# Who makes the high halves: w2's chunks from ScalarE to VectorE, probabilities from tile 16 on from GpSimd to VectorE

## The chip, the cores and the metric

One core of one Trainium2 chip. The metric is the device time of one execution in microseconds (us); for the kernel before it is the median of three runs. The engines are named as the profile names them: PE (TensorE matmul), PEld (its weight load), DVE (VectorE), ACT (ScalarE), POOL (GpSimd) and SP (SyncE, which issues most of the DMAs).

## The reference, cut to what matters

Three stages run one after the other, on a batch of two, with sequence 768 and model width 512. The first is an attention over 8 heads of 64, masked by the equality of hash buckets:

```python
q_bits = (np.einsum('bhsd,dk->bhsk', q, proj) > 0)      # 6 bits, so a bucket number
mask = q_bucket[:, :, :, None] == k_bucket[:, :, None, :]
scores = np.where(mask, scale * q @ k.T, -1e9)
attn = softmax(scores); x = attn @ v
```

The second adds a two-dimensional Fourier transform, normalises and applies a two-layer perceptron: `u = x + real(fft2(x))`, `un = layernorm(u)`, `x = u + relu(un @ w_ch1) @ w_ch2`, where w_ch1 is 512 x 2048 and w_ch2 2048 x 512. The third mixes tokens: `theta = x @ w_theta`, then the sequence sums of `x cos(theta)` and `x sin(theta)` with two 768 x 768 weights, and `u + relu(u @ w_ch)`.

The weights arrive as 64-bit floats, so each weight is first rebuilt as a 32-bit float in the kernel. To keep the accuracy of 32 bits, most operands of a matmul are split into a high half (the value rounded to 16 bits, or to the PE's reduced 32-bit form) and a low half (the value less the high half), and three products are summed. The change concerns who makes high halves.

## The kernel before, in words

**Weights.** `conv16` (line 183) turns a weight into two 16-bit halves, 512 columns at a time. For each chunk `from_f64` (line 169) loads 512 KB of 64-bit words into a buffer `r` (three of them, `NCV`, line 167) by a DMA on SP's queue; ACT runs two operations on it (lines 177 and 179), DVE joins the parts with one scalar_tensor_tensor (line 180, the tile `r` again). Then ACT copies the result into the high half (line 187, `w2h<-r` for w2) and POOL subtracts to get the low half (line 188, `w2l<-r,w2h`). The buffer is free for the next load when POOL is done. w2 has 16 such chunks, each used by the matmuls of one value of `fi` in `mlp2` (line 799).

**Attention of batch 1.** `attention` (line 416) goes over 4 pairs of heads, 2 heads in each, and 6 tiles of 128 query rows in each: 48 tiles, counted by `n`. For a tile, PE makes the scores (`pss`), DVE takes the row maximum (`attn_max`, line 349, a TENSOR_REDUCE into `nm`), ACT takes the exponential (`attn_exp`, line 353) into a 128 x 768 tile of 32-bit floats `p`. `attn_split` (line 361) makes the high half in the tile `p2` on ACT or POOL, by the pattern `h1`, and the low half on POOL (`l1`). A DMA transpose on SP's queue turns both halves (`transposed`, line 379), and PE multiplies them with the values into `pso` (`attn_AV`). Since the buffers of these tiles are shared, the profile names them `p`, `pt` or `x`. The pattern is "aapap", so of each five tiles ACT makes three high halves and POOL two, those with `n % 5` equal to 2 or 4: 19 of the 48.

**Order.** The engines run their instructions strictly in the order in which they were issued. That order comes from the scheduler of the tile framework (line 1178), which plans with modelled durations, the due times set by `at` and `timed` (for w2's chunks 100 us and one more for each, line 968; for the tiles of batch 1 115 us and 2.6 more for each, line 969), and the gates set by `after_gate`. So the two conversions, the tiles of batch 1 and the perceptron of batch 0 (`mlp`, lines 971 and 976) are interleaved: while attention of batch 1 runs, PE also runs `mlp1` and `mlp2` of batch 0, whose evacuations need ACT (`hh<-psm`) and DVE (`hl<-psm,hh`). All instructions that the scheduler places late carry the line of a helper, L62 or L64, so the profile is read by tiles. After the last tile of batch 1 come its Fourier transform, its perceptron and the third stage.

Of the kernel before, what the change touches and what calls it, by code (L numbers as in the profile page):

```python
# [15 lines left out]
AF = mybir.ActivationFunctionType  # L16
# [5 lines left out]
DM, DFF = 512, 2048  # L22
# [15 lines left out]
def run(g):  # L38
    for _ in g:
        pass  # L40
# [30 lines left out]
def fused_kernel(ctx, tc, A, out):  # L71
    nc = tc.nc
    V, AC, PE, PL, SY = (Ordered(tc, e) for e in (nc.vector, nc.scalar, nc.tensor, nc.gpsimd, nc.sync))
# [4 lines left out]
    def mk(p, shape, dt, tag, **kw):  # L78
        return p.tile(shape, dt, tag=tag, name=tag, **kw)
# [4 lines left out]
    def pl_copy(out, in_, scale=1.0):  # L84
        PL.tensor_scalar(out=out, in0=in_, scalar1=scale, scalar2=0.0, op0=ALU.mult, op1=ALU.add)

    def stt(eng, out, in0, in1, op, scale=1.0):
        if eng is V:
            return V.scalar_tensor_tensor(out=out, in0=in0, scalar=scale, in1=in1, op0=ALU.mult, op1=op)
        assert scale == 1.0  # L90
        return eng.tensor_tensor(out=out, in0=in0, in1=in1, op=op)

    T = dict(
        pet='dpd', dup=1, c2=0, c0=46, cx=0, wm=6, gf=1, o2=0, xs=1, sb=2, al=[['p', 2], ['p2', 3], ['pt', 3]], cs='v', g0=1,
        lg=[[0, 2], [2, 4], [4, 6]], ub=2, pace0=1.6, lead=60, f0=50.0, w1=60.0, w1s=1.0, b1=115, pace1=2.6,
        w2=100.0, w2s=1.0, m0=170.0, f1=190.0, th=240.0, m1=290.0, z0=330.0, wt=300.0, n0=8, n1=16, k0=12, k1=16, c1=46, tp=16, i0=40, i1=[20, 10],
        ne=42, es=150, ld='ss', lc='s', ps=[[0, 3], [0, 5], [1, 0], [1, 5]])
# [17 lines left out]
    def PS(k):  # L115
        n = turn[k] % sum(c for _, c in ring[k])
        turn[k] += 1
        for p, c in ring[k]:
            if n < c:
                w = [128, 2, 512] if k == "s" else [128, 512]  # L120
                tag = "psm" if p in [x[0] for x in ring["m"]] else "ps" + k
                live[k] = p.tile(w, F32, tag=tag, name=tag)
                return live[k]
            n -= c
# [4 lines left out]
    def at(us):  # L129

        tc.cur_priority = int(1000 * us)
# [20 lines left out]
    def fill(n, k="o"):  # L152

        for _ in range(n):
            PE.matmul(live[k][:, 392:512], pat[:, 0], pat[:, 1, 0:120], start=True, stop=True)
# [13 lines left out]
    def from_f64(src, scale=1.0, n=CN):  # L169
        p = cvs[turn["cv"] % len(cvs)]  # L170
        turn["cv"] += 1
        r = mk(p, [128, 2 * CN], U32, "r64", bufs=NCV if p is cv_p else None)
        r = r[:, 0:2 * n]
        {"s": SY, "a": AC, "p": PL}[T["lc"]].dma_start(out=r, in_=src.bitcast(U32))
        lo, hi = r[:, 0:2 * n:2], r[:, 1:2 * n:2]

        AC.activation(out=lo, in_=lo, func=AF.Relu, scale=2.0 ** -29 * (1 - 2.0 ** -20), bias=c_half)

        AC.activation(out=f(hi), in_=f(hi), func=AF.Prelu, scale=scale * 2.0 ** -112, alpha=2.0 ** 32)
        V.scalar_tensor_tensor(out=lo, in0=hi, scalar=3, in1=lo, op0=ALU.logical_shift_left, op1=ALU.bitwise_or)  # L180
        return f(lo)

    def conv16(src, n, hi, lo, lo_eng):
        for i in range(n // CN):
            c = slice(CN * i, CN * i + CN)
            w = from_f64(src[:, c], 2.0)
            AC.activation(out=hi[:, c], in_=w, func=AF.Copy)
            stt(lo_eng(i), lo[:, c], w, hi[:, c], ALU.subtract)
            yield

# [28 lines left out]
    def soft_tile(k):  # L219
        n = turn[k] % len(soft[k])  # L220
        turn[k] += 1
        return soft[k][n]
# [116 lines left out]
    def attn_S(st, t):  # L339
        ps = PS("s")  # L340
        c = slice(128 * t, 128 * t + 128)
        for k in range(2):
            for g in range(2):
                mm(ps[:, g, 0:384], st[:, k, c], st[:, 2 + k, 384 * g:384 * g + 384], k == 0, k == 1)
        return ps
# [7 lines left out]
    def attn_exp(ps, nm=None):  # L353
        m = None
        if nm is None:
            nm, m = attn_max(ps)
        p = soft_tile("p")[:, 0]
        e = AC.activation(out=two3(p), in_=ps[:, :, 0:384], func=AF.Exp, bias=nm)
        return p, [m, e]

    def attn_split(p, p2, hi_eng, lo_eng):
        if hi_eng is AC:
            AC.activation(out=p2[:, 0], in_=p, func=AF.Copy)
        else:
            pl_copy(p2[:, 0], p)
        return stt(lo_eng, p2[:, 1], p, p2[:, 0], ALU.subtract)
# [12 lines left out]
    def transposed(p2):  # L379
        pt = soft_tile("pt").bitcast(F16).rearrange("p a n -> p (a n)").rearrange("p (k n) -> p k n", n=128)  # L380
        m = SY.dma_start_transpose(out=pt, in_=p2.bitcast(F16).rearrange("p a n -> p (a n)"))
        return pt, m

    def attn_AV(o, pt, vv, hh, t):
        for k in range(6):
            mm(o[:, t], pt[:, k], vv[:, 0, hh, k], k == 0, False)
            mm(o[:, t], pt[:, k], vv[:, 1, hh, k], False, False)
            mm(o[:, t], pt[:, 6 + k], vv[:, 0, hh, k], False, k == 5)
# [20 lines left out]
    def after_gate(b):  # L409

        es = ExitStack()
        for m in [] if b is None else [b] if hasattr(b, "ins") else gate[b] if isinstance(gate[b], list) else [gate[b]]:
            es.enter_context(tc.issue_after(m.ins))
        return es

    def attention(b, t0, pace, lead, hi_eng, lo_eng, after=lambda b, j: None):
        x_t[b] = mk(x_p, [128, NT, DM], F32, "x")
        n, w = 0, soft["p2"][0].shape[1]
        for j in range(4):
            i = 4 * b + j  # L420
            if i not in made:
                at(t0 + pace * n - lead)
                with after_gate("p1" if b else None):
                    run(prep(b, j))
            st, vv = made[i]
            for hh in range(2):
                h = PO[j] + 4 * hh
                at(t0 + pace * n)
                o = PS("o")[:, 0:NT * (D + 1)].rearrange("p (t d) -> p t d", t=NT)
                for t in range(NT):  # L430
                    at(t0 + pace * n)
                    ps = attn_S(st[hh], t)
                    fill(T["i1"][n] if n < len(T["i1"]) else 0)
                    with after_gate(0 if b and n >= T["n1"] else "ln0" if b and n >= T["n0"] else None):
                        p, m = attn_exp(ps)
                    if not t % w:
                        p2 = soft_tile("p2")
                    with after_gate(0 if b and n >= T["n1"] else None):
                        attn_split(p, p2[:, t % w].bitcast(F16).rearrange("p (a n) -> p a n", a=2), hi_eng(n), lo_eng(n))
                    if t % w == w - 1:  # L440
                        pt, trans = transposed(p2)
                        for i in range(w):
                            attn_AV(o, pt[:, 12 * i:12 * i + 12], vv, hh, t - w + 1 + i)
                    n += 1
                    if j < 3 and [hh, t] in T["ps"]:
                        at(t0 + pace * n - lead)
                        if [hh, t] == T["ps"][0]:
                            new = prep(b, j + 1)
                        next(new)
                at(t0 + pace * n - 30)  # L450
                attn_norm(b, h, o)
            after(b, j)
# [320 lines left out]
    w1, w2 = {}, {}  # L773
# [145 lines left out]
    def timed(gen, t0, dt):  # L919
        n = 0  # L920
        while True:
            at(t0 + dt * n)
            if next(gen, gen) is gen:
                return
            n += 1

    ev = lambda s: [AC if c == "a" else PL if c == "p" else V for c in s]
    h1, l1, c1, c2 = (ev(k) for k in ("aapap", "p", "p", "p"))
    pick = lambda e, last=None: lambda n: last if last and n >= T["ne"] else e[n % len(e)]
    at(0.2)  # L930
    run(prep_pair(0, True))
    at(T["f0"] - 40)
# [32 lines left out]
        timed(take(cw1, T["k1"] - T["k0"]), T["f0"] + 1, T["w1s"])  # L965
    with after_gate(0):
        timed(cw1, T["f0"] + 1, T["w1s"])
        timed(conv16(A["w2"], 16 * DM, w2[0], w2[1], pick(c2)), T["w2"], T["w2s"])
    attention(1, T["b1"], T["pace1"], T["lead"], pick(h1), pick(l1))

    def mlp(b, t0, gs):
        for g in gs:
# [212 lines left out]
```

## Time and profile before

| | us |
|---|---|
| median of 3 runs (729.09 to 731.25) | 729.41 |
| the profiled execution | 728.28 |
| its span, first to last instruction | 726.5 |
| PE busy (matmuls) | 664.8, 92% of the span |
| DVE busy | 402.6, 55% |
| ACT busy | 372.7, 51% |
| POOL busy | 370.1, 51% |

The profiled execution took 1.8 us more than its span, and 1.1 us less than the median. A busy PE is the union of its matmuls, whose ends are modelled, so 92% is an upper bound of its real use. The shares of the other engines are averages over stages: attention and weight conversion fill the first half of the span, the perceptron of batch 1 and the token mixing the second, where PE works almost without a gap and the others idle.

### The profile page before, as it was taken

To read this page: it belongs to the slowest core of one execution; us is meant where nothing else is said; L and a number is where in the kernel's file an instruction comes from. 1 tells how busy PE (TensorE), PEld (TensorE's weight loads), DVE (VectorE), ACT (ScalarE), POOL (GpSimd) and SP (SyncE) were. 2 spreads that over 40 slices of the span, in tenths; PEclk is the share of its full clock that TensorE was granted. 3 is DMA by queue.
4 is the path that set the end of the run, shared out by engine and by line. 5 is a ranking of instruction groups with operands and counts; after the bars stand their busy time and mean duration, and the time that the engine had idled before them with its cause. 6 is when DMAs were issued, how large, how long until landed. Compare 5 with 4: busy or idle time off the path is not lost.

```text
span 726.5 us, 13450 instructions
## 1 busy us (share of the span) xinstructions
PE 664.8 (92%) x5424; PEld 510.9 (70%) x5424; DVE 402.6 (55%) x655; ACT 372.7 (51%) x597; POOL 370.1 (51%) x312
## 2 busy tenths in 40 slices
PE   5798988669668898999999999999999899999998
PEld 2365556557557655786686786687485599999997
DVE  1566787865999665543377583255422476751222
ACT  2565565766988898773423152065325676730010
POOL 3787789586878888776660020033403446930000
PEclk9999999978699999999999999999999999999999
DMA  9896967459889999776560043011004631720202
GB/s 327 186 187 141 157 121 142 93 164 213 197 206 240 269 231 253 151 145 124 102 195 27 13 120 65 1 45 30 1 1 145 223 89 39 234 81 25 88 1 87
DMA packets 161469, 93.68 MB, mean 129 GB/s; under 512 B 137088, under 2 KB 147584, under 8 KB 161408
## 3 DMA queue, kind: packets, MB, share of 16 engines
q1 hardware_dynamic: 159472, 86.27, 51.3%
q0 software_dynamic: 1936, 6.57, 2.6%
q8 instruction: 42, 0.69, 0.4%
q14 instruction: 19, 0.16, 0.1%
HBM read 49.82 MB, written 6.29 MB: 77 GB/s over the span
## 4 chain that ended last, share of the span: by engine, by line
PE 48%; POOL 10%; issue 9%; DMA 6%; ACT 5%; DVE 4%; POOLq 0%; SPq 0%; DVEq 0%; ACTq 0%
PE psm L62 31%; PE psf L62 14%; POOL p L62 3%; ACT r L62 2%; PE pso L62 2%; POOL w1l L62 2%; DMA x<-p 2%; POOL stk L62 2%; PE pss L62 1%; DMA r<-in_wtok 1%; DMA r<-in_w 1%; POOL pt L62 1%; DVE r L62 1%; ACT stk L62 1%; POOL w2l L62 1%
## 5 line engine op out<-in xcount | busy, mean ns | idle before, releaser
L62 PE MATMUL psm<-unT,w1h 128*128 128x256 f16 x768 | 130.4, 274 | 0.1
L62 PE MATMUL psm<-unT,w1l 128*128 128x256 f16 x384 | 105.2, 274 | 0.0
L62 DVE SCALAR_TENSOR_TENSOR r<-r 128x512 uint32<-128x512 uint32 (+1 forms) x64 | 64.6, 1016 | 51.9 <-ACT r L62 49.2
L62 PEld LDWEIGHTS <-w1h 128*128 128x128 f16 (+1 forms) x774 | 75.1, 99 | 15.5 <-issue 4.5
L62 PEld LDWEIGHTS <-hh 128*128 128x128 f16 x384 | 37.1, 98 | 42.8 <-issue 2.2
L62 POOL TENSOR_TENSOR w1l<-r,w1h 128x384 fp32r<-128x384 f32 (+1 forms) x36 | 41.9, 1178 | 43.5 <-ACT w1h L62 43.5
L62 PE MATMUL pss<-stk 128*128 128x384 f32 x192 | 48.8, 384 | 15.2 <-ACT p L62 9.4
L64 PE MATMUL pss<-stk 64*128 64x384 f32 (+1 forms) x288 | 55.4, 470 | 6.4 <-ACT p L64 3.2
L62 DVE TENSOR_REDUCE nm<-pss 128x1 f32<-128x768 f32 x48 | 44.9, 949 | 29.0 <-PE pss L62 28.8
L62 PE MATMUL psm<-w2h,hl 128*128 128x512 f16 x192 | 60.3, 379 | 0.0
L62 PE MATMUL psm<-w2l,hh 128*128 128x512 f16 x192 | 59.8, 379 | 0.2 <-POOL w2l L62 0.2
L62 ACT ACTIVATE r<-r,chalf 128x512 uint32<-128x512 uint32 (+1 forms) x64 | 46.1, 720 | 26.2 <-DMA r<-in_wtok 10.2
L62 PE MATMUL psm<-w2h,hh 128*128 128x512 f16 x192 | 59.3, 379 | 0.0
L62 POOL TENSOR_TENSOR p<-p,p 128x768 f16<-128x768 f32 x32 | 54.7, 1715 | 6.6 <-ACT p L62 5.5
L62 ACT ACTIVATE p<-pss,nm 128x768 f32<-128x768 f32 x48 | 42.5, 892 | 28.1 <-DVE nm L62 23.3
L62 DVE SCALAR_TENSOR_TENSOR hl<-psm,hh 128x512 f16<-128x512 f32 x48 | 32.8, 687 | 41.9 <-ACT hh L62 41.8
L64 DVE TENSOR_REDUCE nm<-pss 128x1 f32<-128x768 f32 x48 | 43.6, 950 | 19.9 <-PE pss L64 19.8
L62 ACT ACTIVATE hh<-psm 128x512 f16<-128x512 f32 x48 | 28.2, 590 | 40.4 <-PE psm L62 40.4
L62 PEld LDWEIGHTS pss<-stk 128*128 128x128 f32 x192 | 34.6, 204 | 20.2 <-ACT p L62 11.9
L62 PEld LDWEIGHTS <-w1l 128*128 128x128 f16 x384 | 37.7, 98 | 5.7 <-issue 1.2
L62 ACT ACTIVATE r<-r 128x512 f32<-128x512 f32 (+1 forms) x64 | 39.5, 618 | 0.0
L62 POOL TENSOR_TENSOR stk<-tt,stk 64x768 fp32r<-64x768 f32 x16 | 31.1, 1945 | 11.5 <-issue 9.6
(322 smaller groups left out, 1552.2 us busy)
## 6 DMA issues: line engine op xcount, KB each, us to landing
r<-in_w SPq DMA_DIRECT2D x32, 512.0 KB, 4.5
r<-in_wtok SPq DMA_DIRECT2D x24, 384.0 KB, 3.8
vr<-in_v SPq DMA_DIRECT2D x8, 390.0 KB, 3.6
stk<-stk SPq DMA_DIRECT2D x16, 192.0 KB, 3.8
xT<-xs SPq DMA_DIRECT2D x12, 256.0 KB, 2.6
xt<-xT SPq DMA_DIRECT2D x4, 768.0 KB, 5.8
ct<-in_ct POOLq DMA_DIRECT2D x4, 579.0 KB, 7.3
sn<-in_sn POOLq DMA_DIRECT2D x4, 576.0 KB, 8.2
```

What stands on the lines that cost most here:

```text
L62: return fn(*a, **k)
L64: self.last = fn(*a, **k)
```

## The change

`conv16` gets a parameter for the engine that makes the high half, and the call for w2 passes VectorE, which makes it by a tensor_copy. w1 keeps ScalarE. `attn_split` gets a branch in which VectorE makes the high half of a tile's probabilities, and the pattern gets a second part: tiles 0 to 15 of batch 1 keep "aapap", and from tile 16 on it is "aavav", so VectorE takes those that GpSimd had. Batch 0's tiles are split by another function call and do not change, nor do the low halves, the buffers, the due times and the DMAs.

```diff
-    def conv16(src, n, hi, lo, lo_eng):
+    def conv16(src, n, hi, lo, lo_eng, by=AC):
         for i in range(n // CN):
             c = slice(CN * i, CN * i + CN)
             w = from_f64(src[:, c], 2.0)
-            AC.activation(out=hi[:, c], in_=w, func=AF.Copy)
+            if by is AC:
+                AC.activation(out=hi[:, c], in_=w, func=AF.Copy)
+            else:
+                by.tensor_copy(out=hi[:, c], in_=w)
             stt(lo_eng(i), lo[:, c], w, hi[:, c], ALU.subtract)
...
         if hi_eng is AC:
             AC.activation(out=p2[:, 0], in_=p, func=AF.Copy)
+        elif hi_eng is V:
+            V.tensor_copy(out=p2[:, 0], in_=p)
         else:
             pl_copy(p2[:, 0], p)
...
-    h1, l1, c1, c2 = (ev(k) for k in ("aapap", "p", "p", "p"))
+    h1, l1, c1, c2 = (ev(k) for k in ("aapapaavav", "p", "p", "p"))
+    high = lambda n: h1[n % 5 + 5 * (n >= 16)]
...
-        timed(conv16(A["w2"], 16 * DM, w2[0], w2[1], pick(c2)), T["w2"], T["w2s"])
-    attention(1, T["b1"], T["pace1"], T["lead"], pick(h1), pick(l1))
+        timed(conv16(A["w2"], 16 * DM, w2[0], w2[1], pick(c2), V), T["w2"], T["w2s"])
+    attention(1, T["b1"], T["pace1"], T["lead"], high, pick(l1))
```

## Rows read from the trace of the kernel before

**Rows 1.** Busy time by stretch: stretch, its us, PE, PEld, DVE, ACT, POOL busy, PEclk, DMA.
```profile
180.00:200.00 20.00, 12.85 (x87) 10.76 (x86) 19.44 (x32) 18.46 (x29) 16.95 (x13) 0.66 0.87 199
200.00:220.00 20.00, 13.65 (x149) 11.39 (x149) 19.46 (x50) 17.71 (x31) 16.15 (x11) 0.91 0.90 218
216.00:252.00 36.00, 32.11 (x326) 26.44 (x323) 28.83 (x34) 30.11 (x46) 31.04 (x21) 0.95 1.12 254
252.00:300.00 48.00, 45.10 (x426) 28.90 (x425) 27.62 (x34) 41.05 (x61) 39.30 (x28) 1.00 1.06 238
320.00:366.00 46.00, 46.00 (x464) 32.59 (x462) 16.19 (x23) 19.42 (x25) 27.66 (x20) 1.00 0.63 118
366.00:726.00 360.00, 354.49 (x2221) 290.34 (x2219) 169.50 (x299) 133.11 (x249) 96.07 (x98) 1.00 0.25 75
216.00:300.00 84.00, 77.21 (x750) 55.34 (x747) 56.45 (x68) 71.16 (x106) 70.34 (x49) 0.98 1.09 245
216.00:320.00 104.00, 96.72 (x968) 71.39 (x965) 67.14 (x83) 85.34 (x125) 86.61 (x60) 0.98 1.01 224
246.00:249.00 3.00, 1.88 (x24) 1.34 (x25) 2.29 (x3) 2.95 (x6) 2.76 (x4) 0.87 1.06 237
249.00:252.00 3.00, 3.00 (x28) 2.63 (x27) 0.00 (x0) 2.94 (x4) 2.67 (x2) 0.56 1.17 269
```

**Rows 2.** Waits of PE, 216 to 320 us: in total, times, longest.
```profile
PE pso L62 <- DMA x<-p: 3.6, 3, 1.9
PE pso L62 <- DMA pt<-pt: 2.7, 3, 1.7
PE pss L62 <- ACT p L62: 0.4, 1, 0.4
PE pso L62 <- DMA pt<-p: 0.3, 1, 0.3
PE psm L62 <- POOL w2l L62: 0.2, 1, 0.2
```

**Rows 3.** Order of time on PE: start, us, what, idle before it and its releaser.
```profile
229.38 0.73 PE L62 MATMUL pso<-vv,x 128*128 128x65 f16 x18 [1.93 <-DMA x<-p]
...
246.72 0.55 PE L62 MATMUL pso<-vv,x 128*128 128x65 f16 x12 [1.14 <-DMA x<-p]
...
277.00 0.73 PE L62 MATMUL pso<-vv,pt 128*128 128x65 f16 x18 [1.70 <-DMA pt<-pt]
```

**Rows 4.** Groups of w2's high halves on ACT: busy us, mean ns, idle before.
```profile
L62 ACT ACTIVATE w2h<-r 128x512 f16<-128x512 f32 x16 | 10.5, 664 | 5.0 <-DVE r L62 5.0
```

**Rows 5.** DVE instructions on tile r, 216 to 300 us: ns min/median/max.
```profile
L62 DVE SCALAR_TENSOR_TENSOR r<-r x19: 679/879/4319, 214.3 to 296.0; 128x512 uint32<-128x512 uint32 x19
```

**Rows 6.** Groups of DVE, 216 to 300 us: busy us, mean ns, idle before.
```profile
L62 DVE SCALAR_TENSOR_TENSOR r<-r 128x512 uint32<-128x512 uint32 x19 | 23.6, 1241 | 13.5 <-ACT r L62 12.0 <-issue 1.0 <-POOL pt L62 0.5
L62 DVE TENSOR_REDUCE nm<-pss 128x1 f32<-128x768 f32 x18 | 16.9, 948 | 8.3 <-PE pss L62 8.1
```

**Rows 7.** Order of time on DVE: one-input 128x512 operations, alone and beside POOL.
```profile
503.57 0.42 DVE L62 TENSOR_SCALAR nn<-rr 128x512 uint32<-128x512 uint32 x1
...
583.66 1.25 DVE L62 TENSOR_SCALAR nn<-rr 128x512 uint32<-128x512 uint32 x1
```

**Rows 8.** Order of time on POOL at 583 us.
```profile
583.53 2.27 POOL L62 TENSOR_TENSOR wtx<-r,wtx 128x384 fp32r<-128x384 f32 x2 [0.20 <-ACT wtx L62]
```

**Rows 9.** POOL's high halves from tile 17 to tile 47: first, sixth and last of 13.
```profile
247.70 1.10 POOL L62 TENSOR_SCALAR p<-p 128x768 f16<-128x768 f32 x1
...
302.83 0.82 POOL L62 TENSOR_SCALAR p<-p 128x768 f16<-128x768 f32 x1
...
360.20 0.83 POOL L62 TENSOR_SCALAR p<-p 128x768 f16<-128x768 f32 x1 [4.03 <-ACT p L62]
```

**Rows 10.** Groups of POOL's high halves, 246 to 366 us: busy us, mean ns, idle before.
```profile
L62 POOL TENSOR_SCALAR p<-p 128x768 f16<-128x768 f32 x9 | 8.0, 889 | 11.3 <-ACT p L62 11.1
L62 POOL TENSOR_SCALAR pt<-p 128x768 f16<-128x768 f32 x4 | 3.3, 832 | 2.1 <-ACT p L62 2.1
```

**Rows 11.** Order of time on DVE and ACT around one chunk of w2.
```profile
240.62 4.32 DVE L62 SCALAR_TENSOR_TENSOR r<-r 128x512 uint32<-128x512 uint32 x1 [0.58 <-ACT r L62]
...
244.98 0.67 ACT L62 ACTIVATE w2h<-r 128x512 f16<-128x512 f32 x1 [2.61 <-DVE r L62]
```

**Rows 12.** Order of time on POOL in the same stretch.
```profile
237.97 3.71 POOL L62 TENSOR_TENSOR stk<-tt,stk 64x768 fp32r<-64x768 f32 x2
241.63 1.64 POOL L62 TENSOR_TENSOR p<-p,p 128x768 f16<-128x768 f32 x1
243.24 1.15 POOL L62 TENSOR_TENSOR w2l<-r,w2h 128x512 f16<-128x512 f32 x1
```

## The prediction

> **What bounds the kernel now.** I read the busy times by stretch first. From 320 us on PE is the bound: it is busy in 46.00 of 46.00 us up to 366, and in 354.49 of 360 after that [rows 1]. Work that any other engine saves there is worth nothing. The change acts from about 216 us, when w2's first chunk is converted, so the stretch that can give something is 216 to 320 us. PE is busy in 96.72 of its 104 us, which leaves 7.3 us of idle PE [rows 1]. The waits of PE there add up to 7.2 us: 3.6 and 2.7 and 0.3 for the transposed probabilities to land, 0.4 for an exponential, 0.2 for w2's low half [rows 2]. So PE waits for the chain that feeds the transposes: scores, maximum on DVE, exponential on ACT, high half, low half on POOL, DMA. In 216 to 300 us ACT is busy in 71.16 of 84 us (85%), POOL in 70.34 (84%), DVE in 56.45 (67%) [rows 1]. The change moves work from the two fuller engines to the emptiest of the three.
>
> **Part 1, w2's 16 chunks.** ACT loses 16 instructions of 664 ns, 10.5 us, and also the 5.0 us in which it stood idle in front of them because DVE had not joined the chunk yet [rows 4]; being in order, it held back the exponentials behind them. The worst case shows it: DVE's join of one chunk took 4.32 us, and ACT waited 2.61 us for it [rows 11]. After the change the copy stands on the engine that made its input, so one change of engine in each chunk's chain (DVE, ACT, POOL) goes.
>
> DVE gains 16 copies of 128x512 from SBUF to SBUF. The trace has no such copy. The nearest row is a one-input DVE operation of the same size: 0.42 us when alone, 1.25 us when a POOL operation was already running [rows 7, 8]. A second reading is DVE's join, right in front of the new copy: 0.68 us at least, 0.88 in the median and 1.24 in the mean, so 0.20 to 0.56 us of waiting each [rows 5, 6]. That gives bounds of 0.42 and 0.98 us (0.42 + 0.56) for the mean, 1.25 for a single bad one. I take 0.70, halfway, because the 0.56 rests largely on the one join of 4.32 us. 16 x 0.70 = 11.2 us on DVE. Queued behind a copy that waits are DVE's row maxima, 18 of them in this stretch [rows 6], for which ACT's exponential and then PE's score buffers wait. POOL's subtraction waits for the copy as it waited for ACT. No DMA is added; the next chunk's load on SP still waits for POOL to free the buffer, so it moves with POOL's end of the chunk.
>
> **Part 2, the probabilities.** Tiles 16 to 47 with n % 5 equal to 2 or 4 are 13; POOL's 13 instructions go, 8.0 + 3.3 = 11.3 us, 0.87 each [rows 10]. DVE gains 13 copies of 128x768. By size from the 0.42 row that is at most 0.42 x 1.5 = 0.63 us alone; the same number of elements in a maximum takes 0.95 [rows 6], which is the upper bound alone. I take 0.63 and the same 0.28 of waiting as above (0.70 less 0.42): 0.91 each. Only five of the 13 lie in front of 300 us, the sixth is at 302.83 and the last at 360.20 [rows 9]. The last eight run where POOL waits (4.03 us in front of the last one), DVE is busy in 16.19 of 46 us and PE is full [rows 1, 9]: I cost them at nothing. Their cover is PE's queue of matmuls of batch 0's perceptron; without it each would give 0.2 us (0.63 for 0.83) or cost 0.4 (the 1.23 of the last rival for 0.83).
>
> **The sum.** In 216 to 300 us ACT falls to 60.7 us (72%), POOL to 70.34 - 5 x 0.87 = 66.0 (79%), and DVE rises to 56.45 + 11.2 + 5 x 0.91 = 72.2 (86%). Of PE's 7.2 us of waiting, the 1.93 us at 229.38 [rows 3] is left: its probabilities were made before the change reaches far. The other 5.3 us can shorten. I let each of these waits shrink by what a chain gains, about one POOL high half or one ACT queue place, 0.87 us. Of the two longer than that, 1.14 and 1.70 [rows 3], 0.27 and 0.83 stay, so 5.3 - 1.1 = 4.2 us go. Against this I set one DVE copy held by POOL in front of a maximum on the path, 1.25 us. Net gain 4.2 - 1.25, some 3.0 us. The profiled execution took 728.28 us for a span of 726.5, and the sum makes it 725.3. The median of the runs stands 1.1 us above it, so 729.41 - 3.0 = **726.4 us**.
>
> The lower bound of the stage is all 5.3 us, and one thing more: from 246 to 252 the granted clock falls to 0.87 and 0.56 in two rows of 3 us, which is 3.4 us at the lower level (1.2 GHz for 2.4), right after PE's 1.14 us of idle [rows 1, 3]. If the gap goes and the clock stays, half of that, 1.7 us, is won: 729.4 - 7.0 = 722.4.
>
> The order in which instructions stand on each engine is planned anew with the changed durations. The trace can't show what that does; its bounds are the 5.5 us of idle PE after 366 us [rows 1] below, and nothing that I can price above. I put it into the width.
>
> **Rivals.**
>
> *No change.* PE's order of matmuls is fixed and nearly full from 252 us on (45.10 of 48, then the rows above), and the waits that are left end with a DMA landing. The DMA engines' busy share is 1.12 and 1.06 in 216 to 300 us, against 0.63 after 320 [rows 1]. Faster halves only make loads and transposes start earlier into full queues. Against it: not all of the waits fall into the fullest stretch. Time: 729.4, with 2.2 us to either side, 0.3%, about what a measurement of this kernel can tell from no change. It would also come so if the planner simply put the copies where they delay as much as they save.
>
> *DVE becomes the bound, slower.* The place is DVE's queue from 216 to 300 us. What a full DVE does stands in the rows: in 180 to 220 us it is busy in 19.44 and 19.46 of 20 us, and PE only in 12.85 and 13.65, at a clock of 0.66 and 0.91 [rows 1]. What would fill it is waiting for POOL. POOL held DVE in the 1.25 us row: DVE's operation began at 583.66, 0.13 us after the first of two POOL operations, and ended at 584.91, just past the middle of their 2.27 us (584.67) [rows 7, 8]. The join of 4.32 us spans three POOL operations without a pause [rows 11, 12]. If each copy meets POOL's load in full, it waits for half a mean operation (70.34 / 49 = 1.44 us, half 0.72) in 84% of cases, 0.60 us: 1.02 for a chunk and 1.23 for a tile. DVE then needs 56.45 + 16.3 + 6.2 = 79.0 of 84 us, 94%. I take 90%, 75.6 us, as the point where the others start to wait, nearer to the full rows than to the 67% of now. The 3.4 us above it stretch the stage by 3.4 / 0.9 = 3.8 us: 733.2. It decides from a mean of 0.81 us for the chunks' copies on ((75.6 - 56.45 - 6.2) / 16). Against it: the copy follows the join, which has often just waited for POOL, and POOL itself loses work.
>
> The Trainium skill's page "SBUF — State Buffer", section "Who interferes with whom", states this rule: a VectorE copy that runs in a two-port mode takes a port pair shared with GpSimd for its whole length, and whichever comes second waits until the other is done. By that rule the last case is the one to expect, 733.2 us. The trace agrees on the wait (0.42 against 1.25 us) [rows 7] but does not show how often the copies will meet POOL.
>
> **How the numbers follow.** I give the gain 0.40, no change 0.33, DVE as the bound 0.27. Faster by over 0.3% is the first case, within 0.3% the second, slower the third. The gain alone would range from 722.4 to 727.2. The range for all is 723.0 to 733.5: it leaves out the last of the gains and that half of the third case in which copies wait longer than I priced.
>
> **What would show it.** Right, if ACT shows no wait for DVE's join in front of w2's high half, POOL's instructions fall by 13, DVE's copies average about 0.70 us, the stretch from 216 to 320 us loses some 3 us of idle PE, and everything after has the same length. Wrong, if the copies average above 0.81 us and the exponentials wait for row maxima behind them, or if PE's gaps for transposes stay while ACT and POOL get emptier; or if the time moves in a stretch that the change doesn't touch, which would point to the new order.

## The result, and the profile after the change

The changed kernel takes 740.41 us in the median of four runs (734.3 to 741.47), the kernel before in the same comparison 730.33. The ratio is 1.0123, 95% interval [1.0075, 1.0171]: slower by about 9 us, where the forecast was 3 us faster and the range ended at 733.5. The profiled execution took 741.47 us for a span of 739.7, against 728.28 and 726.5; it is the slowest of the four, and 728.28 lies below every timed run of the kernel before, so the two profiles stand somewhat further apart than the medians.

Busy time by stretch, kernel after (columns as in [rows 1], here with their heading):

```profile
core 0: us, PE busy (x) PEld busy (x) DVE busy (x) ACT busy (x) POOL busy (x), PEclk, DMA share, GB/s
216.00:300.00 84.00, 72.07 (x680) 49.89 (x680) 70.42 (x86) 59.39 (x85) 62.28 (x43) 0.98 1.08 235
216.00:320.00 104.00, 91.00 (x877) 65.18 (x876) 84.91 (x103) 70.81 (x100) 75.34 (x50) 0.98 1.00 211
320.00:366.00 46.00, 44.15 (x432) 30.34 (x430) 18.54 (x28) 23.67 (x30) 24.14 (x16) 1.00 0.78 127
366.00:384.00 18.00, 17.25 (x225) 14.82 (x224) 7.14 (x13) 4.32 (x7) 6.98 (x6) 1.00 0.47 74
```

The same view of the kernel before, for the stretch that [rows 1] does not have:

```profile
366.00:384.00 18.00, 17.77 (x182) 15.29 (x181) 15.32 (x26) 3.90 (x8) 10.49 (x17) 1.00 0.61 199
```

In 216 to 300 us the busy times of the three other engines came near the sum: DVE 70.42 us (foretold 72.2), ACT 59.39 (60.7), POOL 62.28 (66.0). PE did not follow. In 216 to 320 us it is busy for 91.00 us where [rows 1] has 96.72, and from 320 to 366 us, full before, it has gaps again: 44.15 of 46. Up to 384 us that makes 152.40 busy us against 160.49, 8.1 less. The granted clock is the same 0.98 and 1.00 in both.

The waits of PE, kernel after, 216 to 384 us (in total, times, longest):

```profile
PE pss L62 <- ACT p L62: 4.7, 6, 1.8
PE pso L62 <- DMA pt<-pt: 4.6, 6, 1.8
PE pss L62 <- DVE bits L62: 4.1, 2, 3.2
PE pso L62 <- DMA pt<-p: 0.9, 1, 0.9
PE psm L62 <- DVE w2h L62: 0.8, 1, 0.8
PE pso L62 <- DMA x<-p: 0.7, 1, 0.7
PE psm L62 <- DVE hl L62: 0.3, 1, 0.3
```

They add up to 16.1 us. The kernel before has 7.2, and they are those of [rows 2], since none comes after 320 us. The wait for score buffers (`pss`, behind an exponential) has grown from 0.4 to 4.7 us, and 4.1 us for the bucket bits are new; the waits for transposes have changed places, not gone (6.2 us, 6.6 before). The last tile's values of batch 1 show what has gathered, by the order of time on PE, before and after:

```profile
368.21 0.73 PE L62 MATMUL pso<-vv,x 128*128 128x65 f16 x18
```

```profile
380.72 0.72 PE L62 MATMUL pso<-vv,x 128*128 128x65 f16 x18
```

12.5 us later, nearly all of the 13.2 us between the two profiled executions.

The groups of DVE, kernel after, 216 to 300 us (busy us, mean ns, idle before):

```profile
L62 DVE SCALAR_TENSOR_TENSOR r<-r 128x512 uint32<-128x512 uint32 x18 | 21.1, 1172 | 10.9 <-ACT r L62 6.8 <-POOL p L62 2.8 <-POOL stk L62 1.3
L62 DVE TENSOR_REDUCE nm<-pss 128x1 f32<-128x768 f32 x17 | 16.0, 943 | 0.4 <-PE pss L62 0.4
L62 DVE CAST w2h<-r 128x512 f16<-128x512 f32 x16 | 15.0, 939 | 0.3
...
L62 DVE CAST p<-p 128x768 f16<-128x768 f32 x3 | 4.6, 1535 | 1.9 <-ACT p L62 1.0 <-DMA x<-p 0.9
...
L62 DVE CAST pt<-p 128x768 f16<-128x768 f32 x2 | 2.7, 1362 | 0.0
```

The chunks' copies average 0.94 us, not 0.70, and lie above the 0.81 from which the third case was to decide. The five copies of probabilities in this stretch average 1.46 us, not 0.91. One place shows a long wait on DVE reach PE. The order of time on DVE, then PE, kernel after:

```profile
240.24 3.94 DVE L62 SCALAR_TENSOR_TENSOR r<-r 128x512 uint32<-128x512 uint32 x1 [1.31 <-POOL stk L62]
244.21 0.43 DVE L62 CAST w2h<-r 128x512 f16<-128x512 f32 x1
244.56 0.94 DVE L62 TENSOR_SCALAR bits<-pss 64x768 bf16<-64x768 f32 x1
...
245.56 0.98 PE L62 MATMUL pss<-stk 128*128 128x384 f32 x4 [3.17 <-DVE bits L62]
```

A join held by POOL, a copy and then the bits: PE stood for 3.17 us. But the join of [rows 11] was as long (4.32 us), and PE did not wait for it, because other work stood in its order there. Was the DVE copy the cause, or the order around it?

### The profile page after: what moved, and what is told of

It reads as the page before. It is cut to its first block, busy times and chain, and to the rows that moved or that the text cites. A ratio compares the mean times of both kernels' runs of the same rounds, so it can differ in the third digit from the quotient of the medians.

```text
span 739.7 us, 13463 instructions
## 1 busy us (share of the span) xinstructions
PE 667.2 (90%) x5424; PEld 510.0 (69%) x5424; DVE 426.6 (58%) x684; ACT 364.8 (49%) x581; POOL 359.1 (49%) x299
## 4 chain that ended last, share of the span: by engine, by line
PE 42%; DMA 10%; issue 9%; POOL 8%; DVE 7%; ACT 7%; SPq 0%; POOLq 0%; DVEq 0%; ACTq 0%
PE psm L62 27%; PE psf L62 13%; ACT r L62 2%; DMA pt<-pt 2%; DMA r<-in_w 2%; POOL w1l L62 2%; ACT stk L62 2%; POOL p L62 2%; DMA r<-in_wtok 2%; DMA pt<-p 2%; PE pso L62 1%; PE pss L62 1%; DMA r<-in_wch 1%; POOL w2l L62 1%; ACT p L62 1%
## 5 line engine op out<-in xcount | busy, mean ns | idle before, releaser
L62 DVE TENSOR_REDUCE nm<-pss 128x1 f32<-128x768 f32 x48 | 45.0, 946 | 16.2 <-PE pss L62 16.1
```

The lines of the kernel that those rows point to most:

```text
L62: return fn(*a, **k)
```

## The experiments

The order of every engine is planned by a scheduler with modelled durations. With the copies on another engine, and so with other modelled durations, it came out differently on every engine, on PE in 1453 of 5296 places, from about 200 us on. So two theories stand:

- **A, the copies.** They are slow beside POOL and delay maxima, exponentials and scores (the prediction's third case).
- **B, the order.** What is slow is the order planned anew, whoever makes the high halves.

They can be taken apart by building a program twice: the first build, with one division of work, gives each engine's order; the second, with the other division, is held to it wherever both programs have the instruction on the same engine (the first two lines are shortened):

```diff
+    order = program(plan)                 # engine -> sequence of instructions
+    nc = program(real, order)
...
+        for e in ENGINES:
+            last = None
+            for k in seq[e]:
+                if where[k] != e:
+                    continue
+                if last is not None:
+                    tc.add_manual_dep(traced[k], traced[last].name, NoSync, reason="order")
+                last = k
```

Moved instructions go where the scheduler puts them between the others. What the holding itself costs was not measured apart; held kernels at 1.0023 and 1.0025 below leave it little room. The ratio is always to the kernel before, in the same comparison.

**Work against order.** `plan` = the old division, `real` = all 29 copies on DVE:

> All 29 copies on VectorE as in the change, but every other instruction keeps, on its engine, the place that it has in the kernel before. Theory A (VectorE's copies meet GpSimd and hold up VectorE's queue): as slow as the changed kernel, 738 to 743 us, copies of w2 averaging 0.9 us or more in 216 to 300 us. Theory B (the new order of the instructions makes the loss): near the kernel before, 727 to 732 us.

And `plan` = the changed division, `real` = the old one:

> The work is divided as in the kernel before (w2's high halves on ScalarE, probabilities on ScalarE and GpSimd), but all instructions that are common to both kernels stand in the order of the changed kernel. Theory A: near the kernel before, 728 to 733 us. Theory B: 737 to 743 us.

The copies in the old order: 733.12 us, 1.0047 [1.0027, 1.0068], 1.1 us above B's range and 4.9 below A's. The old work in the new order, without one copy on DVE: 740.64 us, 1.0158 [1.0126, 1.0189], as slow as the changed kernel and inside B's range. Busy time by stretch of the first, then of the second:

```profile
216.00:300.00 84.00, 73.22 (x673) 51.99 (x673) 71.66 (x87) 59.00 (x85) 63.67 (x42) 0.96 1.02 235
216.00:320.00 104.00, 93.22 (x893) 68.23 (x893) 83.49 (x104) 72.52 (x103) 76.91 (x50) 0.97 0.94 213
320.00:366.00 46.00, 46.00 (x480) 32.24 (x478) 20.59 (x31) 23.47 (x29) 24.60 (x16) 1.00 0.69 130
```

```profile
216.00:320.00 104.00, 92.55 (x882) 66.78 (x881) 63.92 (x78) 79.48 (x116) 77.94 (x56) 0.95 0.97 210
320.00:366.00 46.00, 43.98 (x411) 29.54 (x409) 15.94 (x23) 22.79 (x30) 28.89 (x20) 1.00 0.67 118
```

The longest waits of PE in the second, 216 to 384 us, and the one that ends with DVE:

```profile
PE pso L62 <- DMA pt<-pt: 7.1, 5, 3.1
PE pss L62 <- ACT p L62: 5.5, 4, 2.0
...
PE pss L62 <- DVE bits L62: 0.4, 1, 0.4
```

DVE's 63.92 us are less than the old order's 67.14 [rows 1], and only 0.4 us of PE's waits ends with DVE, so a fuller DVE is not what held PE; and the stretch from 320 to 366 us is full in the old order and has some 2 us of gaps in the new one, with or without the copies. The main loss is B's. A is real and smaller: 0.47% of 729.41 are 3.4 us. The granted clock does not follow the time: in 216 to 320 us it is 0.98 both before and after the change, and 0.97 and 0.95 in these two.

**A copy that POOL cannot hold.** The copy written as a maximum over an axis of length one, all 29 of them, in the new order and in the old one (shown for the chunks, shortened):

```diff
-                by.tensor_copy(out=hi[:, c], in_=w)
+                V.tensor_reduce(out=hi[:, c], in_=w.unsqueeze(2), axis=AX.X, op=ALU.max)
```

> The changed kernel, instruction for instruction in the same order, but its 29 copies on VectorE are made by a reduction over an axis of length 1, which computes the same. Theory A1 (the copies are slow because they wait for GpSimd operations, and GpSimd for them): if this form does not wait, each 128x512 copy takes some 0.69 us whatever GpSimd does (against a mean of 0.94), and the time falls by 3 to 8 us to 732 to 737. Theory A2 (VectorE simply has too much in its queue, waiting or not): 738 to 743 us. Theory B: 738 to 743 us.

> The order of the kernel before, copies on VectorE by the reduction over an axis of length 1. Theory A1: faster than the copies proper in the same order by 3 to 8 us. Theory B: 727 to 732 us, like the copies proper in this order.

Measured: 739.67 us, 1.0120 [1.0066, 1.0174], in the new order, outside A1's range; 731.31 us, 1.0023 [0.9995, 1.005], in the old one, 1.8 us below the copies proper where A1 had 3 to 8. The copies of w2's chunks by tile (ns min/median/max, first and last start), as casts in the old order, then as reductions in the old order:

```profile
L62 DVE CAST w2h<-r x16: 411/892/2039, 216.2 to 290.1; 128x512 f16<-128x512 f32 x16
```

```profile
L62 DVE TENSOR_REDUCE w2h<-r x16: 668/677/689, 214.1 to 285.8; 128x512 f16<-128x512 f32 x16
```

Their groups, 216 to 300 us (busy us, mean ns, idle before):

```profile
L62 DVE CAST w2h<-r 128x512 f16<-128x512 f32 x16 | 17.4, 1090 | 0.2
```

```profile
L62 DVE TENSOR_REDUCE w2h<-r 128x512 f16<-128x512 f32 x15 | 10.1, 678 | 0.2
```

The cast takes 0.41 us at least and up to 2.04 with POOL busy for 63.67 of the 84 us; the reduction takes longer than the shortest cast, but always 0.67 to 0.69. The Trainium skill, page "SBUF — State Buffer", section "Who interferes with whom", says that casts can take the port pair shared with GpSimd and that `tensor_reduce` on trn2 never does; these two lines agree. By the two ratios the steady copy gives back half of A's loss, but the intervals overlap (from 1.0027 to 1.005), so that size stays open. In the new order it gives nothing that can be told: of PE's 16.1 us of waits there, 0.8, in one wait, end with such a copy (`w2h`).

**The two parts, each in the old order and in its own.** Against the changed kernel, first w2 alone, then the probabilities alone, each held to the old order and then planned freely (what the edits come to):

```diff
-    h1, l1, c1, c2 = (ev(k) for k in ("aapapaavav", "p", "p", "p"))
+    h1, l1, c1, c2 = (ev(k) for k in ("aapapaapap", "p", "p", "p"))
```

```diff
-        timed(conv16(A["w2"], 16 * DM, w2[0], w2[1], pick(c2), V), T["w2"], T["w2s"])
+        timed(conv16(A["w2"], 16 * DM, w2[0], w2[1], pick(c2)), T["w2"], T["w2s"])
```

> Only w2's 16 copies go to VectorE, GpSimd keeps the probabilities, and every instruction keeps its place from the kernel before. What is in dispute is where the 3.5 us of the run with all 29 copies in the old order come from. Theory B (the order is the main loss, the copies themselves cost little): with the copies averaging about 0.94 us (as in the changed kernel) they put 16 x 0.94 = 15 us on VectorE inside 216 to 300 us and nearly all of the 3.5 us is here: 732 to 733 us. Rival (the probabilities' copies are the dear ones, since five of them stand right in front of a transpose that TensorE waits for): this kernel is within 0.3% of the kernel before, 728 to 731 us.

> Only the 13 copies of the probabilities go to VectorE, ScalarE keeps w2's, and every instruction keeps its place from the kernel before. Theory B: VectorE gains only about 5 x 1.4 = 7 us before 300 us and has room for it (56.5 + 7 of 84 us), so the time is within 0.3%: 728 to 731 us. Rival (these copies are the dear ones): 732 to 733 us.

> Only w2's 16 copies go to VectorE, and the order of all engines is planned anew for it, as it was for the changed kernel. Theory B, the new order: a plan made anew can come out well or badly, so this may lie anywhere from 727 to 741 us; if it lies over 4 us from the run of the same work in the old order, the plan has done that. Rival (theory A, the copies themselves): it equals the run of the same work in the old order within 0.3%.

> Only the 13 copies of the probabilities go to VectorE, and the order is planned anew. Theory B, the new order: anywhere from 727 to 741 us, whatever the old order gave for the same work. Theory A (the copies themselves): it equals the run of the same work in the old order within 0.3%.

And later the old work in the two orders planned for the parts:

> The kernel before's division of work, in the whole order that was planned for w2's copies alone on VectorE. Theory R (any order that is planned anew for this stage comes out about 1% behind the one that the kernel before has, whatever the copies do): 734 to 741 us. Rival S (the orders are as good as the old one and only the moved copies make them slow; the whole new order was one unlucky draw): 728 to 732 us.

> The kernel before's division of work, in the whole order that was planned for the probabilities' copies alone on VectorE. Theory R: 733 to 741 us; the copies alone, in the old order, gave 1.0025, and in this order 1.0083, so the order alone should give about 1.006, some 735 us. Rival S: 728 to 732 us.

| copies on DVE | in the old order | in the order planned for them | old work in that order |
|---|---|---|---|
| w2 | 734.15, 1.0091 [1.0058, 1.0124] | 737.70, 1.0135 [1.0093, 1.0177] | 739.11, 1.0138 [1.0106, 1.0170] |
| probabilities | 730.36, 1.0025 [0.9999, 1.0051] | 734.50, 1.0083 [1.0056, 1.0110] | 738.15, 1.0148 [1.0086, 1.0211] |
| both | 733.12, 1.0047 [1.0027, 1.0068] | 740.41, 1.0123 [1.0075, 1.0171] | 740.64, 1.0158 [1.0126, 1.0189] |

Read down: in the old order w2's copies carry A's price, the probabilities' copies cost nothing that can be told; 1.0091 for w2 alone and 1.0047 for both have intervals that overlap. Read the last two columns: in each order that was planned anew, the kernel with the copies cannot be told from the old work; its medians are even a little lower. The right column alone is B. Against the expectations: w2 alone in the old order came out 1.15 us above B's range, and in its own order only 3.6 us later, short of the 4 that were to show the plan at work; the probabilities' own order is 4.1 us later, and the old work in it, at 738.15, 3 us later than the 735 that R had worked out. Both runs of the old work lie in R's ranges and outside S's.

**Which engine's order?** The old work, once with only PE's order from the changed kernel, once with only the other four engines' (ACT, DVE, POOL, SP); and all copies on DVE with only PE's order from the kernel before. The engines left free are planned anew (shortened):

```diff
-    order = program(plan)
+    order = {e: s if e in HELD else [] for e, s in program(plan).items()}
```

> The kernel before's division of work (ScalarE and GpSimd make the high halves), with only TensorE's order taken from the changed kernel; the other engines' orders are planned freely around it. What is open is which part of the new order is slow. Theory P (TensorE's own order: it has fewer matmuls of batch 0's perceptron in front of a tile's values and so meets transposes that have not landed): as slow as the kernel before's work in the whole new order, 737 to 741 us. Rival Q (the order on the other engines: a chunk's work put in front of a maximum or an exponential): 728 to 732 us.

> The kernel before's division of work, with the orders of ScalarE, VectorE, GpSimd and the DMA-issuing SyncE taken from the changed kernel; TensorE's order is planned freely around them. Theory P (TensorE's order): 728 to 732 us. Rival Q (the others' order): 737 to 741 us.

> All 29 copies on VectorE, with only TensorE's order taken from the kernel before; the other engines' orders are planned freely around it. Theory P (TensorE's order is what is slow in the changed kernel): close to the same copies in the whole old order, 731 to 735 us, the copies' own price being left. Rival Q (the others' order): 737 to 741 us, like the changed kernel. If the freely planned engines fit the moved work better than the old order did, it may come out at or below the kernel before, 727 to 730 us; that would be a version worth keeping.

Measured: 739.89 us, 1.0133 [1.0103, 1.0163]; 740.45 us, 1.0147 [1.0119, 1.0175]; 737.15 us, 1.0097 [1.0066, 1.0128]. P has the first and misses the second, Q the reverse, and the third lies at the lower edge of Q's numbers. So these runs single out neither PE's order nor the others'. In each of the three some engines were planned afresh, which is what they share, and that gave theory R: leaving the old order costs, for whatever reason it is left.

**A new order for a reason that has nothing to do with the copies.** The kernel before with one number of the plan changed:

```diff
-        ... pace0=1.6, lead=60, ... b1=115, pace1=2.6,
+        ... pace0=1.6, lead=55, ... b1=115, pace1=2.6,
```

> The kernel before with one planning number changed that has nothing to do with the copies: the scores of batch 1 become due 55 instead of 60 before their values; the division of work is untouched and every engine's order is planned anew. Theory R: slower, 733 to 742 us. Rival S: within 0.5% of the kernel before, 727 to 733 us.

and with the pace instead:

```diff
-        ... lead=60, ... b1=115, pace1=2.6,
+        ... lead=60, ... b1=115, pace1=2.8,
```

> The kernel before with the pace of batch 1's tiles planned at 2.8 instead of 2.6, which changes TensorE's order in some 50 places and no other engine's order. Theory R in its strict form (any change of the plan costs): 733 us or more. Rival: a change of so few places leaves the time within 0.3%, 728 to 732 us, and the loss grows with how much of the stage is planned anew.

740.08 us, 1.0148 [1.0114, 1.0182], and 729.54 us, 1.0014 [0.9985, 1.0043]. As planned, the first differs from the kernel before in 1968 of PE's 5296 places; the second in 45, and, other than expected, in three places each on ACT and SP as well. Busy time by stretch of the two (the second from an execution of 733.9 us, 4.4 above its median):

```profile
216.00:320.00 104.00, 91.77 (x886) 67.26 (x887) 71.37 (x107) 83.26 (x121) 80.87 (x58) 0.95 1.00 214
320.00:366.00 46.00, 44.86 (x468) 32.64 (x469) 16.54 (x24) 22.22 (x28) 28.81 (x20) 1.00 0.71 126
```

```profile
216.00:320.00 104.00, 96.34 (x930) 70.63 (x927) 68.44 (x82) 82.78 (x121) 83.33 (x59) 0.95 0.96 218
320.00:366.00 46.00, 46.00 (x483) 32.34 (x480) 16.19 (x23) 21.79 (x27) 29.29 (x22) 1.00 0.65 121
```

The first has no changed instruction and nearly the changed kernel's PE time (91.77 and 44.86 against 91.00 and 44.15); the second, with an order hardly touched, has the old one's (96.72 and 46.00). So B holds in R's form, and R's strict form, that any touch costs, falls. What PE waits for in the first, 216 to 384 us, the four largest:

```profile
PE pss L62 <- ACT p L62: 4.5, 3, 2.3
PE pso L62 <- DMA x<-p: 3.0, 1, 3.0
PE psm L62 <- DVE rs L62: 2.7, 1, 2.7
PE pso L62 <- DMA pt<-p: 2.5, 3, 1.1
```

Three of the four belong to the attention chain again, at other places than in the changed kernel; the wait for `rs` is for the layer norm of batch 0.

**More draws for the changed kernel.** Last, the changed kernel with another `lead`: 55, 65 and 50.

```diff
-        ... lead=60, ... b1=115, pace1=2.6,
+        ... lead=55, ... b1=115, pace1=2.6,
```

> The changed kernel with the scores of batch 1 due 55 instead of 60 before their values, so that every order is planned anew once more. Theory R (any order planned anew lies 1.3 to 1.6% behind the one that the kernel before has, the copies adding little to it): 737 to 743 us. Rival D (orders are draws with a wide spread, and the old one is merely a good one): anywhere from 725 to 745 us, and one of the three draws of this batch at or below 731 us, which would be a version worth keeping.

> The changed kernel with the scores of batch 1 due 65 instead of 60 before their values. Theory R: 737 to 743 us. Rival D: anywhere from 725 to 745 us.

> The changed kernel with the scores of batch 1 due 50 instead of 60 before their values. Theory R: 737 to 743 us. Rival D: anywhere from 725 to 745 us.

744.42 us, 1.0206 [1.0145, 1.0266]; 737.54 us, 1.0097 [1.0065, 1.0129]; 736.19 us, 1.0078 [1.0047, 1.0110]. R's band of 737 to 743 us was too narrow at both ends, and none of the draws reaches the kernel before. D's wide range holds all three, but the draw at or below 731 us that it foretold did not come. With the first draw (1.0123) the orders planned for the changed division spread over some 1.3%, more than the copies cost in any one order. No version here beats the kernel before.

## Why the prediction was wrong

**The step that failed** is the one on the order: "nothing that I can price above. I put it into the width." The sum took the old order for granted. What the order costs alone, measured with the old work, is 1.58% [1.26, 1.89], some 11.5 us; it was given no rival, no chance and no price of its own. The text came near a sign for it ("if the time moves in a stretch that the change doesn't touch"). The stretch from 320 to 366 us has copies of the change, but they were costed at nothing since PE was full; it lost 1.85 us of PE, and the old work in the new order, without the copies, lost 2.02 there. So the cover named there, PE's queue of batch 0's perceptron, depends on the order too.

**Near, in part by luck: the load on the engines.** 13 high halves left POOL, ACT's and DVE's busy times in 216 to 300 us came within 1.8 us of the sum, POOL's within 3.7. But DVE's copies took 22.3 us there (15.0 + 4.6 + 2.7) where the sum had 15.8; its total came near because its other work in the stretch fell from 56.45 to 48.1 us, which the sum did not foresee. And ACT's 5.0 us of waiting in front of w2's high half [rows 4] did not turn into gain: its idle time in front of the exponentials, 216 to 300 us, grew from 3.2 to 11.2 us, before and after:

```profile
L62 ACT ACTIVATE p<-pss,nm 128x768 f32<-128x768 f32 x18 | 16.0, 886 | 3.2 <-DVE nm L62 3.1
```

```profile
L62 ACT ACTIVATE p<-pss,nm 128x768 f32<-128x768 f32 x17 | 15.3, 898 | 11.2 <-DVE nm L62 9.0 <-DVE r L62 2.2
```

**Wrong: the gain.** PE's waits did not shorten by 4.2 us; they grew to 16.1 up to 384 us. In the old order, where the sum can be checked as it was meant, the time rose by 3.4 us instead of falling by 3.0. The probabilities alone, in the old order, are at 1.0025 [0.9999, 1.0051]: no gain either.

**Mis-sized: the copies.** 0.70 us was halfway between 0.42 and 0.98; they take 0.94 in the new order and 1.09 in the old one, just under the upper bound and past it. The lower end was right: 0.41 at least. The probabilities' copies were put at 0.91 and take 1.46 in the new order and 0.84 in the old one. Halfway was the wrong choice where POOL is busy for 84% of the stage [rows 1]; the case that met POOL by chance and for half an operation had 1.02.

**The third case, DVE as the bound**, priced a chunk's copy well (1.02 us for 1.09) and gave 733.2 us, where the copies in the old order measured 733.12. That the times agree so closely is luck: DVE was to be busy for 79.0 of 84 us, and is for 71.66 (85%), below the 90% from which the others were to wait; and w2's copies alone came out at 734.15. The exponentials did wait for the maxima behind the copies: in the groups of ACT, 216 to 300 us, old order with the copies, then the old work in the new order:

```profile
L62 ACT ACTIVATE p<-pss,nm 128x768 f32<-128x768 f32 x17 | 15.2, 894 | 10.7 <-DVE nm L62 10.1 <-DVE r L62 0.4
```

```profile
L62 ACT ACTIVATE p<-pss,nm 128x768 f32<-128x768 f32 x17 | 15.2, 894 | 0.1
```

But the second kernel, with 0.1 us of such idle time, is the slower one. And the reductions in the old order, at 731.31 us, have nearly as much of it as the copies proper:

```profile
L62 ACT ACTIVATE p<-pss,nm 128x768 f32<-128x768 f32 x18 | 16.1, 895 | 9.7 <-DVE nm L62 9.1 <-POOL p L62 0.5
```

So this wait alone does not set the time, and this case is not the main reason why the changed kernel is slow. It would have been easy to stop there: the copies are above 0.81 us, ACT waits for maxima, the kernel is slower, and all of that is true.

**Open** is what the old order has that the others lack. In the orders planned anew that are shown here PE waits at different places, mostly for the same chain, and neither PE's order nor that of the others was shown to be the one at fault. Nor is it shown how the old order's planning numbers were chosen: if by measured times, out of many, then most other orders would be expected to come out behind it.

## What to carry to other kernels

Where a scheduler lays out the order from modelled durations, a change of division is two changes, the work and the order, and their costs can differ by a factor of three: hold the order and swap the work, then hold the work and swap the order, before a wait in the new trace is called the cause. Price a new order from other orders of the old work (one planning number that should not matter, here worth 1.5%), and give it a chance of its own in a forecast. A stage in which PE is full can be full only in that order.

## What the runs showed that was not expected

A 128x512 cast on DVE varies five-fold in a stretch with POOL busy for 76% (0.41 to 2.04 us), while the same copy as a reduction over an axis of length one varies by 3% (0.668 to 0.689): the operation that is slower at its best is quicker in the mean (0.68 against 1.09 us). For the five 128x768 copies there it is not so: 0.94 us as a reduction, 0.84 as a cast. And one planning number that changes no instruction moved the kernel by 1.48% [1.14, 1.82], with DVE busy for 69%, ACT for 80% and POOL for 78% of the 104 us to 320 us: none of the three was full, and the time was lost in the order.
